# Feature derivatives written in place, and the key and value gradients of layer 0 transposed by DMA

## The chip, the cores and the metric

The kernel runs on one core of a Trainium2 chip. The metric is the device time of one launch in microseconds (us), as the median of several runs. Engines are named as in the profile: PE is TensorE's matmul (PEld its weight load), DVE is VectorE, ACT is ScalarE, POOL is GpSimd, SP is SyncE, which here issues every DMA. L983 means line 983 of the kernel before.

## The reference

A stack of four pre-norm attention layers over 2048 tokens of width 640 (32 heads of 20), and its whole backward pass. Layers 0 and 2 (kind A) are linear attention, layers 1 and 3 (kind B) sliding-window softmax attention with a window of 256. Kind A, cut to what matters:

```
phi = lambda t: where(t > 0, t + 1, exp(t)) + 1e-6
pq, pk = phi(q), phi(k)
kv  = einsum("bhsd,bhse->bhde", pk, v);  z = sum of pk over s
num = einsum("bhqd,bhde->bhqe", pq, kv); den = einsum("bhqd,bhd->bhq", pq, z) + 1e-6
o   = num / den;   x = x + o @ wo      (input of each layer is layernorm(x))
```

Outputs are the result and the gradients of x and of the four weight matrices. The derivative of phi can be had from its stored value: it is exp(t) for t below zero and 1 above, so it equals min(phi - 1e-6, 1). The gradients of q and k before phi are the gradients behind it times that derivative.

## The kernel before

Tokens are cut into 16 tiles of 128 rows. The program runs forward, then the backward pass of layer 3, layer 2, layer 1 and layer 0; the weight gradients (products over all 2048 tokens of two layers, `weight_jobs`) fill in from the end of layer 1 on and then run alone until the end.

The order of the work on PE, DVE, ACT and POOL is written out by hand. Each step of a tile has a place, a number of slots; the step at place a of tile t goes into slot 8t + a (rounded down), and the slots are emitted one after the other, so that steps of neighbouring tiles interleave. Every engine takes its instructions in that order. The DMAs on SP's queue are ordered by the compiler's scheduler, and SP too is in order: a DMA that waits holds up those behind it. PSUM tiles come from a ring of six buffers in order of allocation.

`plan_linear` holds the backward pass of a linear layer for one tile. It is used twice: for layer 2 (with `by_pe` = 0), and for layer 0 (with `by_pe` = 4), where after each slot `fill(0.8)` emits 0.8 us worth of weight-gradient products (eight of 240 columns). The list `PLACES["l2"]` gives its places: first the load, then the steps in the order of `fs`. The steps of a tile are:

- load (for two tiles at once): `ldn`, `lv`, `lpqk` (stored features phi(q) and phi(k)), `lhn`, `lg`, two buffers each;
- `turn`: transposes on PE of `ldn`, `lv` and the key half of `lpqk`, evicted by DVE (`dnT`) and ACT (`vT`, `pkT`);
- `part`: products per half of the heads. For q ("dn") and k ("v") DVE forms the derivative `fd` from `lpqk` (L969) and multiplies the PSUM result by it into `dqa` (L971), two instructions for each of four halves; for v ("pk") ACT copies (L966). `dqa` is the tile's gradient of q, k and v, 128 x 1920, with two buffers;
- `turn_q`, `turn_kv(1)`, `turn_kv(2)`: `dqa` is transposed into `dqT` (three buffers). The q third goes by a DMA transpose, apart from tiles 0 to 3 of layer 0, where PE does it (L921). The k and v thirds go by PE, five transposes each (L983), evicted by DVE (L986) and ACT (L988). Behind the last, `dqa` is stored;
- `dh`: 30 products of `dqT` with the turned weights, for each half first the k third, then v, then q; ACT evicts (L1001);
- `ln`, `ln2`: the layer norm's backward: DVE (L1009, L1011), POOL (L1012), ACT (L1018), POOL (L1019), and for every second tile a store of `lgn`.

The softmax here doesn't subtract the row's maximum and nothing guards it: scores larger than these inputs give would overflow.

## Time and profile before

| What | Value |
|---|---|
| Median of 7 runs | 2253.94 us (2244.75 to 2260.27) |
| The profiled execution | 2250.06 us |
| Its span, first to last instruction | 2248.3 us |
| Mean granted PE clock | 0.981 |
| PE busy over the span | 2073.9 us (92%) |
| DVE, ACT, POOL busy | 1455.0 (65%), 1357.4 (60%), 1091.1 us (49%) |
| Layer 2, backward | about 1168 to 1285 us |
| Layer 0, backward, with weight gradients between | about 1815 to 2030 us |
| Weight gradients alone | about 2030 us to the end |

A row of a group of instructions names the line, the engine, the operation, the tile written and those read, the shapes and the count, then busy time and the mean of one. In the timeline a row has start, duration, the instruction, and in brackets the idle time before it and what ended that. Matmul ends are modelled, so that start to start is the better measure of what a matmul takes in a stream.

### The profile page before, as it was taken

To read this page: it belongs to the slowest core of one execution; us is meant where nothing else is said; L and a number is where in the kernel's file an instruction comes from. 1 tells how busy PE (TensorE), PEld (TensorE's weight loads), DVE (VectorE), ACT (ScalarE), POOL (GpSimd) and SP (SyncE) were. 2 spreads that over 40 slices of the span, in tenths; PEclk is the share of its full clock that TensorE was granted. 3 is DMA by queue.
4 is the path that set the end of the run, shared out by engine and by line. 5 is a ranking of instruction groups with operands and counts; after the bars stand their busy time and mean duration, and the time that the engine had idled before them with its cause. 6 is when DMAs were issued, how large, how long until landed. Compare 5 with 4: busy or idle time off the path is not lost. (4 is left out here: it accounts for less than half of the span.)

```text
span 2248.3 us, 76829 instructions
## 1 busy us (share of the span) xinstructions
PE 2073.9 (92%) x32061; PEld 1692.7 (75%) x32061; DVE 1455.0 (65%) x2934; ACT 1357.4 (60%) x2109; POOL 1091.1 (49%) x1888
## 2 busy tenths in 40 slices
PE   7889998899989999998879989999988899999999
PEld 5667776577767877776657768777776788889998
DVE  6788885777745788887749858788876245540000
ACT  5468887377776888887636668888876234430000
POOL 2056665156666677777534456777775312220000
PEclk9999999999999999999999989999999999999999
DMA  7498875698878599998789733999997998857753
GB/s 260 141 241 226 227 224 150 164 223 220 207 217 223 150 185 208 212 213 174 149 284 256 211 98 93 202 209 208 209 188 171 271 303 246 252 152 199 202 142 90
DMA packets 721357, 449.50 MB, mean 200 GB/s; under 512 B 461296, under 2 KB 697840, under 8 KB 720624
## 3 DMA queue, kind: packets, MB, share of 16 engines
q1 hardware_dynamic: 721008, 444.58, 78.4%
q8 instruction: 251, 4.11, 0.8%
q14 instruction: 98, 0.80, 0.1%
HBM read 213.09 MB, written 149.82 MB: 161 GB/s over the span
## 5 line engine op out<-in xcount | busy, mean ns | idle before, releaser
L665 DVE TENSOR_TENSOR ds<-dp,e 128x768 bf16<-128x768 f32 (+2 forms) x512 | 463.7, 906 | 173.2 <-PE s L138 60.6
L662 ACT ACTIVATE e<-s 128x768 bf16<-128x768 f32 (+2 forms) x512 | 395.6, 773 | 136.2 <-PE s L138 100.0
L385 ACT ACTIVATE eT<-sT 128x1536 bf16<-128x1536 f32 (+2 forms) x256 | 351.1, 1371 | 130.1 <-PE sT L138 128.8
L138 PE MATMUL wg<-rhs,lhs 128*128 128x240 bf16 (+1 forms) x3840 | 377.2, 257 | 10.1 <-DMA lhs<-o 7.1
L138 PEld LDWEIGHTS <-lhs 128*128 128x128 bf16 x3840 | 340.7, 99 | 22.6 <-DMA lhs<-o 8.2
L674 POOL TENSOR_SCALAR_AFFINE_SELECT e<-e 128x256 bf16<-128x256 bf16 x512 | 208.0, 408 | 249.5 <-ACT e L662 242.3
L138 PEld LDWEIGHTS <-dqT 128*128 128x128 bf16 x1920 | 170.7, 98 | 63.2 <-issue 10.4
L391 POOL TENSOR_SCALAR_AFFINE_SELECT eT<-eT 128x512 bf16<-128x512 bf16 x256 | 162.7, 637 | 107.6 <-ACT eT L385 105.9
L138 PE MATMUL acc<-slabqs,ds 128*128 128x20 bf16 x2880 | 210.2, 172 | 1.9 <-ACT dq L744 0.5
L138 PE MATMUL dp<-slabvT,dT 32*128 32x384 bf16 (+2 forms) x1024 | 168.1, 321 | 44.5 <-DVE ds L665 39.5
L138 PE MATMUL acc<-ds,e 128*128 128x20 bf16 x2880 | 208.2, 171 | 0.0
L138 PEld LDWEIGHTS <-ds 128*128 128x128 bf16 x2880 | 187.9, 96 | 12.2 <-issue 3.9
L678 POOL TENSOR_SCALAR_AFFINE_SELECT e<-e 128x256 bf16<-128x256 bf16 x448 | 196.9, 440 | 0.0
L138 PEld LDWEIGHTS <-e 128*128 128x128 bf16 x2880 | 170.1, 96 | 10.9 <-issue 2.1
L1012 POOL TENSOR_TENSOR dh<-dh,lg 128x640 f32<-128x640 f32 x32 | 51.5, 1610 | 255.6 <-DVE s L1009 255.6
L685 PE MATMUL flip<-ident,ds 128*128 128x128 bf16 x1944 | 170.1, 221 | 3.3 <-DVE ds L772 1.2
L138 PE MATMUL s<-slabkT,slabqT 32*128 32x384 bf16 (+2 forms) x1024 | 168.2, 324 | 4.6 <-ACT dT L797 3.3
L1094 DVE CAST wr<-wg 128x240 bf16<-128x240 f32 (+1 forms) x72 | 27.2, 377 | 223.9 <-PE wg L138 211.5
L1092 ACT CAST wr<-wg 128x240 bf16<-128x240 f32 (+1 forms) x48 | 16.3, 339 | 257.3 <-PE wg L138 243.7
L138 PE MATMUL dense<-WB,hnT 128*128 128x320 bf16 x960 | 164.0, 302 | 3.9 <-DVE o L459 2.4
L138 PE MATMUL dense<-WTA,dqT 128*128 128x320 bf16 x960 | 160.9, 298 | 1.9 <-DMA dqT<-dqa 1.6
L138 PE MATMUL acc<-slabks,dsT 128*128 128x20 bf16 x2880 | 147.0, 171 | 12.2 <-DMA dsT<-ds 12.2
(176 smaller groups left out, 4599.7 us busy)
## 6 DMA issues: line engine op xcount, KB each, us to landing
rhs<-dqkv SPq DMA_DIRECT2D x64, 480.0 KB, 4.9
s<-s SPq DMA_DIRECT2D x32, 768.0 KB, 3.9
T<-T SPq DMA_DIRECT2D x32, 768.0 KB, 3.9
dqkv<-dq SPq DMA_DIRECT2D x16, 960.0 KB, 5.8
dqkv<-dqa SPq DMA_DIRECT2D x32, 480.0 KB, 5.0
slabkT<-T SPq DMA_DIRECT2D x56, 256.0 KB, 4.4
slabvT<-T SPq DMA_DIRECT2D x56, 256.0 KB, 3.8
slabks<-s SPq DMA_DIRECT2D x56, 256.0 KB, 3.7
```

Of the source, the lines that this page charges most:

```text
L138: return self.nc.tensor.matmul(out, lhsT=lhsT, rhs=rhs, start=start, stop=stop, skip_group_check=True, **kw)
L385: nc.scalar.activation(e[:, :, 0:nb * P], s[:, :, 0:nb * P], ACT.Exp)
L391: nc.gpsimd.affine_select(out=dg, in_=dg, compare_op=ALU.is_ge, fill=0.0, base=0, pattern=[[0, 4], [1, P]], channel_multiplier=-1)
L662: nc.scalar.activation(u.e[:, :, 0:u.cw], s[:, :, 0:u.cw], ACT.Exp)
L665: nc.vector.tensor_tensor(out=d.ds[:, :, 0:d.cw], in0=d.dp[:, :, 0:d.cw], in1=d.e[:, :, 0:d.cw], op=ALU.mult)
L674: nc.gpsimd.affine_select(out=dg, in_=dg, compare_op=ALU.is_ge, fill=0.0, base=0, pattern=[[0, 2], [-1, P]], channel_multiplier=1)
L678: nc.gpsimd.affine_select(out=fr, in_=fr, compare_op=ALU.is_ge, fill=0.0, base=-1, pattern=[[0, 2], [1, P]], channel_multiplier=-1)
L685: nc.tensor.transpose(ps[:, 3 * j + i, :], f.ds[:, j, i * P:(i + 1) * P], self.ident)
L1012: nc.gpsimd.tensor_tensor(out=x["dh"], in0=x["dh"], in1=L["g"][:, i, :], op=ALU.add)
L1092: nc.scalar.copy(o[:, 0:w], ps[:, 0:w])
L1094: nc.vector.tensor_copy(o[:, 0:w], ps[:, 0:w])
```

## The change

In `part` the two-instruction form for q and k becomes one multiplication by the loaded feature tile, which by then holds the derivative. A new step `slope` turns the q half and the k half of `lpqk` into derivatives in place, one instruction of 640 columns each, at places 0.05 and 0.1. Since that overwrites phi(k), the transposes of phi(k) move from place 1.2 to place -0.6, ahead of those of `lv`. The constant `one` goes. In layer 0, from tile 4 on, `turn_kv` issues a DMA transpose from SP's queue in place of five PE transposes and an eviction, and the places of `dh`, `ln` and `ln2` of these tiles move back by five slots.

```diff
-    l2=[-10.4, -1.3, 0.6, 1.2, 1.9, 3.2, 4.6, 6.2, 7, 7.5, 5, 8, 8.3, 10.2, 11.8, 14, 14.4, 15.4, 16, 16.2, 18.7],
+    l2=[-10.4, -1.3, 0.6, -0.6, 1.9, 3.2, 4.6, 6.2, 7, 7.5, 5, 8, 8.3, 10.2, 11.8, 14, 14.4, 15.4, 16, 16.2, 18.7, 0.05, 0.1],
...
-        self.one = const.tile([P, 1], BF, name="one")
-        nc.gpsimd.memset(self.one, 1.0)
...
-                f = lp.le.tile([P, CW], BF, name="fd")
-                nc.vector.scalar_tensor_tensor(out=f, in0=src("pq" if nm == "dn" else "pk")[:, c * CW:(c + 1) * CW], scalar=-EPS,
-                                               in1=self.one.to_broadcast([P, CW]), op0=ALU.add, op1=ALU.min)
-                nc.vector.tensor_tensor(out=dst, in0=ps[:, 0:CW], in1=f, op=ALU.mult)
+                nc.vector.tensor_tensor(out=dst, in0=ps[:, 0:CW], in1=src("pq" if nm == "dn" else "pk")[:, c * CW:(c + 1) * CW], op=ALU.mult)
+
+        def slope(nm):
+
+            nc.vector.tensor_scalar(out=src(nm), in0=src(nm), scalar1=-EPS, scalar2=1.0, op0=ALU.add, op1=ALU.min)
...
         def turn_kv(j):
+            if lp.by_pe and t >= 4:
+                self.dma(x["dT"][:, j * DT:(j + 1) * DT, :], x["dqkv"][:, j * D:(j + 1) * D], transpose=True)
+                if j == 2:
+                    self.dma(self.rows(self.dq[l], t), x["dqkv"])
+                return
...
-        fs += [lambda n=n, ci=ci: dh(n, ci) for ci in range(2) for n in range(3)] + [ln, ln2]
+        fs += [lambda n=n, ci=ci: dh(n, ci) for ci in range(2) for n in range(3)] + [ln, ln2, lambda: slope("pq"), lambda: slope("pk")]
+        if lp.by_pe and t >= 4:
+            a = a[:13] + [v + 5 for v in a[13:21]] + a[21:]
```

In the built program PE has 120 matmuls fewer, DVE 76 instructions fewer, ACT 12 fewer and SP 24 DMA transposes more.

## The prediction

> **What bounds the kernel now.** I read the page's busy times first (PE 92% of the span), then the chain of work that ended last, then busy time by stretch for the two stages that the change touches, then their timelines and groups. From about 1853 us on, the chain is PE alone (start, length, work):

> ```profile
> 1877.36 1.64 PE wg L138 x16
> 1879.00 1.52 PE dense L138 x14
> ...
> 1890.50 1.64 PE wg L138 x16
> 1892.14 1.52 PE dense L138 x14
> ```

> The pattern repeats every 13.14 us: one tile of layer 0 with 64 weight-gradient products in it. Busy time by stretch, layer 0 from tile 4 on and then layer 2 (us, each engine's busy time with its count, granted clock, DMA share, GB/s):

> ```profile
> 1853.00:2010.70 157.70, 157.70 (x1718) 140.66 (x1717) 89.66 (x170) 62.88 (x130) 37.09 (x24) 1.00 0.79 218
> 1181.90:1283.00 101.10, 94.76 (x1103) 75.94 (x1102) 94.48 (x180) 69.82 (x140) 45.72 (x32) 1.00 0.86 234
> ```

> In layer 0 PE never idles and DVE is at 57%. In layer 2 DVE is busy as long as PE, 94.5 of 101.1 us, and PE idles 6.3. The PE timeline of layer 2 shows why:

> ```profile
> 1230.59 0.51 PE L162 MATMUL flip<-ident,ldn 128*126 128x128 bf16 x6
> ...
> 1237.73 0.51 PE L162 MATMUL flip<-ident,ldn 128*126 128x128 bf16 x6
> ...
> 1239.53 0.32 PE L138 MATMUL dense<-dmz,pkT 120*128 120x40 bf16 x4 [0.45 <-DVE dqa L971]
> ```

> A tile takes 7.1 to 7.3 us there (from 1179.92 to 1252.22 the same row comes ten times further on, 7.23 us each), and in each a product waits for a PSUM buffer that DVE empties late. Without a wait a tile takes 6.58 us: two of the ten intervals are that long (1179.92 to 1186.50, 1216.68 to 1223.26), and the layer 0 tile gives the same, 13.14 less 64 products at 0.82/8 us.

> DVE is late because of L969. Its groups in layer 2:

> ```profile
> L969 DVE SCALAR_TENSOR_TENSOR fd<-lpqk,one 128x320 bf16<-128x320 bf16 x56 | 47.4, 846 | 0.0
> L971 DVE TENSOR_TENSOR dqa<-dense,fd 128x320 bf16<-128x320 f32 x55 | 27.0, 492 | 5.5
> ```

> L969 is half of DVE's busy time. Alone it takes 0.48 us; where POOL's sums L1012 or L1019 run it takes 1.1 to 1.8 us and ends some 0.35 us after POOL does (1237.55 + 1.33 = 1238.88; POOL's ended at 1238.53). L971 is 0.49 us whether POOL runs or not.

> **Derivative in place.** Removed per tile: 4 x 0.846 = 3.4 us of DVE. Added: two instructions of 128x640 with one bf16 source. No such row exists; the nearest are L417 (same size, bf16, 435 to 447 ns, up to 741) and L560 (half the size, in place, 244 ns). I take 0.44 each, 0.9 a tile, and for the bounds 0.23 and 1.5 us each (stretched by POOL as L969 was; at slot 8t POOL is idle in layer 2, as it waits for L1009 behind them). DVE's load falls from 94.48/14 = 6.75 to about 4.3 us a tile, well below 6.58, so the PSUM wait goes. The multiplication reads the same sizes: no change. In layer 0 the freed 2.5 us a tile is worth nothing: PE waits for DVE nowhere in the stretch.

> What is late next in layer 2? Three candidates. (a) DVE now has to wait, in `slope` of k, for PE's transposes of phi(k); behind it are L1009 and the evictions. Those transposes stand a slot earlier on PE (place -0.6 against 0.1), and DVE's previous instruction, the eviction L986, already waits for later PE work; cost 0. (b) The eviction L986 has less PE work to hide behind, since the phi(k) transposes no longer stand there: k-v transposes start at 0, eviction runs from 0.48 to 0.97 us (1897.16, 1897.64, 1898.13 in layer 0), and its reader can come at 0.55 + 0.34 + 0.15 = 1.04 us. It just fits: 0 to 0.1 us a tile. (c) The q transpose. For odd tiles SP's queue has it behind the store of `lgn`, and that ends the chain L1009, L1012, L1018, L1019. Before: L1019 ends at 1238.53, the transpose is issued at 1239.02, lands 3.7 us later (the stage's median) at about 1242.7, and is read by the products at 1243.46: 0.7 us to spare. The two slopes stand ahead of L1009 and push the chain back by 0.9, less some 0.2 that DVE gains; the reader comes 0.5 us earlier in a shorter tile (six slots of eight). So it is about 0.5 us late in every odd tile. The even tiles' transposes wait for the multiplications only, which come over 1 us earlier. The phi(k) load has about 9 us of slack and needs 1.6.

> Sum for layer 2: 14 tiles x (7.23 - 6.58) = 9.1 us, less 7 x 0.5 for (c), about 6 us. Bounds: 9.5, and 2 if (c) costs a full microsecond in every odd tile.

> **Key and value gradients by DMA, layer 0.** Removed from PE: 12 tiles x 10 transposes. In the stream ten take 0.55 us from start to start, not the modelled 0.72:

> ```profile
> 1897.16 0.72 PE L983 MATMUL flip<-ident,dqa 128*128 128x128 bf16 x10
> 1897.71 0.51 PE L162 MATMUL flip<-ident,lv 128*126 128x128 bf16 x6
> ```

> 12 x 0.55 = 6.6 us, all on the path, as PE is never idle there. The weight products are a fixed total, so five more slots at the end only move them. The evictions L986 (0.49) and L988 (0.69 us) that go were beside PE's work: 0.

> Added: 24 transposes on SP's queue and the DMA engines. SP takes 1.24 us for one (median of the q ones), 2.5 us of a 12.6 us tile; behind them stand the `dqa` store, loads and the stores of weight gradients, whose tiles have slack. The new wait is of the first `dh` product for the k third. In the built order I counted PE's work between the last product that feeds a k or v transpose, with all that stands ahead of it on SP, and the reader: at least 11 us at the durations above. Needed: about 0.75 us on DVE or ACT, 1.2 to 3.7 of SP, and the landing, whose row is

> ```profile
> DMA to landing us min/median/max: 2.6/4.1/7.1
> ```

> At the median that is hidden; with the longest landing and three transposes in a row (0.75 + 3.7 + 7.1 = 11.6) it is 0.6 us late. So the DMA engines decide. One transpose alone, in a DMA window of 1.2 us (672 packets, 640 of them its own):

> ```profile
> q1 hardware_dynamic: 672, 0.16, 68.7%
> ```

> 0.687 x 1.2 = 0.82 us of all 16 engines; 24 make 20 us. Amid other traffic the packets of one took up to 2.8 us of engine time in the trace's records, but that includes sharing. The stage has 0.79 x 157.7 = 124.6 us; with 20 more, 144.4 in 157.7 - 6.6 = 151.1 us, a share of 0.96; from 1900 to 1920 us the share is 1.10 with PE busy for all 20 us. I take 0.5 us lost in all (one late landing), 6 us won. Bounds: 6.6 won, and the loss below.

> [...]

> **Sum.** 6 + 6 = 12 us off 2250.06 (the profiled execution, 1.8 of it outside the span) is 2238; the median of the runs stands 3.9 above that execution, so 2253.94 - 12 = 2242.

> **Rivals.**
> *Both in full* (part of my case): 9.1 + 6.6 = 15.7 us, 2238.
> *One gain is taken by a new wait* (0.19): either (c) costs a microsecond or more, so that the transposes replace DVE as the bound of layer 2, or the k and v transposes are late by 0.5 us a tile in layer 0. Then 6 us are left: 2248, at the edge of "same". For it: four waits for `dqT` already (3.5 us) in layer 2. Against: the even tiles' transposes come earlier.
> *The DMA engines become the bound of layer 0* (0.08), the other side. The stage then takes 124.6 + 24 x C us. Above C = 1.1 us it exceeds PE's 151.1; at C = 2.0 it eats layer 2's gain too, and above that the kernel is slower. At 2.5, near what transposes took amid traffic, it is 184.6 us, 27 longer than now, less 6: 2275. For it: a share of 0.79 already, small packets. Against: 0.82 alone.
> *The change doesn't do what it says*: excluded by the built order (120 PE transposes and 76 DVE instructions fewer, 24 DMA transposes more).

> **How the numbers follow.** Forecast 0.73 (2234 to 2247), one gain lost 0.19 (2245 to 2252), DMA bound 0.08 (2250 to 2280). About 0.3%, 6.8 us, is what a measurement of this kernel can tell from no change. Faster: 0.73 and a little of the second case, 0.75. Same: the rest of the second and a little of the third, 0.16. Slower 0.09. Range 2233 to 2253: down to both gains in full with the medians' scatter, up to the second case.

> **What would show it.** Right: `ldn` transposes of layer 2 some 6.6 to 6.9 us apart with no wait for `dqa L971`; tiles of layer 0 12.6 us apart with PE busy throughout; slopes at about 0.44 us. Wrong: PE waiting for `dqT<-dqa` in either stage for more than some 5 us, a DMA share near 1.1 over the whole of layer 0, or a longer wait for `lhs<-o` behind it (2.0 us now).

## The result and the profile after

| | Before | After |
|---|---|---|
| Median of the runs, same chip | 2253.8 us | 2243.16 us (2236.06 to 2245.81) |
| Ratio of after to before, 95% interval | | 0.9947 [0.9935, 0.9960] |
| The profiled execution | 2250.06 us | 2243.45 us |
| Its span | 2248.3 us | 2241.7 us |
| Mean granted clock | 0.981 | 0.976 |

The kernel is faster by 0.53%, 11.9 us by the ratio (9.0 to 14.7). The forecast was 12 us. The sum came out; the experiments show that its two terms did not. The gain in layer 0 was sized wrongly, and the runs give the other part more than its 6 us.

First the two stretches of before again, in the kernel after (us, busy time of PE, PEld, DVE, ACT, POOL with counts, granted clock, DMA share, GB/s; layer 2 first):

```profile
1181.90:1283.00 101.10, 97.05 (x1129) 78.38 (x1128) 57.83 (x154) 69.84 (x143) 41.45 (x32) 1.00 0.86 235
1853.00:2010.70 157.70, 157.70 (x1667) 140.30 (x1664) 56.00 (x136) 56.24 (x121) 35.25 (x24) 1.00 1.00 249
```

In layer 2 DVE goes from 94.48 busy us to 57.83. PE still idles 4 of 101 us, but for another reason. What its products waited for in these 101 us (total, times, longest), before:

```profile
PE dense L138 <- DVE dqa L971: 4.8, 11, 0.5
...
PE dense L138 <- DMA dqT<-dqa: 1.6, 2, 1.1
```

and after:

```profile
PE dense L136 <- DMA dqT<-dqa: 4.0, 5, 1.6
```

The wait for DVE's multiplication is gone, and the wait for the q transposes has grown. In layer 0 PE is busy throughout as before, while the DMA share goes from 0.79 to 1.00. Since PE doesn't wait there, the spacing of the tiles tells the gain. The chain of waits, where before had 13.14 us from one pattern to the next:

```profile
1881.11 1.64 PE wg L136 x16
1882.75 1.52 PE dense L136 x14
...
1893.72 1.64 PE wg L136 x16
1895.37 1.52 PE dense L136 x14
```

1893.72 - 1881.11 = 12.61 us. The PE timeline of layer 2:

```profile
1201.95 0.51 PE L160 MATMUL flip<-ident,ldn 128*126 128x128 bf16 x6
...
1208.69 0.51 PE L160 MATMUL flip<-ident,ldn 128*126 128x128 bf16 x6
...
1211.05 0.88 PE L987 MATMUL flip<-ident,dqa 128*128 128x128 bf16 x10
1211.77 0.51 PE L160 MATMUL flip<-ident,lv 128*126 128x128 bf16 x6
...
1215.41 0.85 PE L136 MATMUL dense<-WTA,dqT 128*128 128x320 bf16 x5 [1.33 <-DMA dqT<-dqa]
...
1216.94 0.51 PE L160 MATMUL flip<-ident,ldn 128*126 128x128 bf16 x6
```

A tile of 6.74 us, then one of 8.25, in which the `dh` products wait for the q transpose. Five such waits, of 0.16 to 1.6 us and all in odd tiles, make the 4.0 us. DVE's groups in layer 2, the multiplication (L971 before, L966 in the kernel after) and the new slope:

```profile
L966 DVE TENSOR_TENSOR dqa<-dense,lpqk 128x320 bf16<-128x320 f32 x56 | 25.6, 485 | 9.7 <-PE dense L136 9.6
...
L970 DVE TENSOR_SCALAR lpqk<-lpqk 128x640 bf16<-128x640 bf16 x28 | 7.7, 318 | 0.0
```

The multiplication is as it was (485 against 492 ns); the slope takes 318 ns, not the 440 I had put in.

What layer 0 gives is partly taken back behind it. The weight gradients alone begin with a gap on PE, for left operands (`lhs`) that have not landed. The PE timeline there, before:

```profile
2069.94 6.24 PE L138 MATMUL wg<-rhs,lhs 128*128 128x160 bf16 x64 [2.01 <-DMA lhs<-o]
```

and after:

```profile
2060.25 0.45 PE L136 MATMUL wg<-rhs,lhs 128*128 128x160 bf16 x4 [0.72 <-DMA lhs<-o]
2062.06 0.45 PE L136 MATMUL wg<-rhs,lhs 128*128 128x160 bf16 x4 [1.36 <-DMA lhs<-o]
2063.79 2.45 PE L136 MATMUL wg<-rhs,lhs 128*128 128x160 bf16 x17 [1.28 <-DMA lhs<-o]
```

In brackets is the idle time ahead of each row and what ended it: 2.0 us in one piece before, 3.4 in three after. (By starts, so with the weight load that waits first, PE's gap is 2.24 us before and 4.05 after; gaps below are meant so.)

At the border of layer 2 and layer 1 PE waits some 3 us once, in both kernels, but before ahead of layer 1's first pair of `s` products (its attention scores) and after ahead of the second. Before:

```profile
1296.48 0.29 PE L138 MATMUL s<-slabkT,slabqT 32*128 32x128 bf16 x2 [3.27 <-ACT dT L797]
```

and after:

```profile
1295.55 0.29 PE L136 MATMUL s<-slabkT,slabqT 32*128 32x128 bf16 x2 [3.07 <-ACT e L660]
```

So layer 2 is measured to the second pair, behind this wait in both. By stage (start to start of named PE products, one profile each, us):

| | Before | After |
|---|---|---|
| Layer 2: first `ldn` transpose to layer 1's second pair of `s` products | 134.4 | 131.3 |
| Layer 1: from there to the first weight product | 466.1 | 467.2 |
| Layer 0: first `ldn` transpose to last `dh` | 217.75 | 214.56 |
| From there to the last weight product | 218.9 | 216.1 |

Other profiles with the same instructions in layer 2 as after have 127.9 to 131.3 us for it. So a single profile settles a stage to a few us only, and the verdicts below are by the ratios of many runs, with the traces for the mechanism.

### The profile page after: what moved, and what is told of

It is laid out like the page before. It is cut to its first block, busy times and chain, and to the rows that moved or that the text cites. A ratio compares the mean times of both kernels' runs of the same rounds, so it can differ in the third digit from the quotient of the medians.

```text
span 2241.7 us, 76479 instructions
## 1 busy us (share of the span) xinstructions
PE 2076.0 (93%) x31941; PEld 1693.7 (76%) x31941; DVE 1374.1 (61%) x2858; ACT 1347.6 (60%) x2097; POOL 1082.8 (48%) x1887
## 5 line engine op out<-in xcount | busy, mean ns | idle before, releaser
L136 PE MATMUL wg<-rhs,lhs 128*128 128x240 bf16 (+1 forms) x3840 | 377.4, 257 | 11.5 <-DMA lhs<-o 9.0
L136 PEld LDWEIGHTS <-lhs 128*128 128x128 bf16 x3840 | 340.2, 99 | 26.3 <-DMA lhs<-o 10.4
L136 PEld LDWEIGHTS <-dqT 128*128 128x128 bf16 x1920 | 170.9, 98 | 65.9 <-issue 10.4
L136 PEld LDWEIGHTS <-ds 128*128 128x128 bf16 x2880 | 187.9, 96 | 12.6 <-issue 4.4
L1016 POOL TENSOR_TENSOR dh<-dh,lg 128x640 f32<-128x640 f32 x32 | 44.8, 1399 | 245.0 <-DVE s L1013 168.4
L136 PE MATMUL dense<-WTB,dqT 128*128 128x320 bf16 x960 | 155.6, 302 | 0.0
```

The source lines that it names most:

```text
L136: return self.nc.tensor.matmul(out, lhsT=lhsT, rhs=rhs, start=start, stop=stop, skip_group_check=True, **kw)
L1016: nc.gpsimd.tensor_tensor(out=x["dh"], in0=x["dh"], in1=L["g"][:, i, :], op=ALU.add)
```

## The experiments

The theory going in: the slopes free DVE, which gives layer 2's gain; the q transposes are the next wait there, as part (c) of the prediction has it; in layer 0 the gain is PE's, with transposes hidden by the five slots' lead, and some of it is lost in the gap behind it. The rivals: the two parts give other shares than 6 and 6 (e1, e2); the q transposes are late for the slopes (e3), for the store ahead of them on SP's queue (e11, e12, e13), or for their landing alone; those of layer 0 are hidden without the lead too (e4), or only just (e6); the gap is noise (e8 to e10). All ratios are to the kernel before on the same chip.

**Each part alone.** e1_slope is the kernel after without the second part:

```diff
-            if lp.by_pe and t >= 4:
+            if lp.by_pe and t >= 99:
                 self.dma(x["dT"][:, j * DT:(j + 1) * DT, :], x["dqkv"][:, j * D:(j + 1) * D], transpose=True)
...
-        if lp.by_pe and t >= 4:
-            a = a[:13] + [v + 5 for v in a[13:21]] + a[21:]
```

> The derivative in place alone (both layers), the k and v thirds of dqa still transposed on PE, dh at its old places. Theory (two separate gains, about 5 us in layer 2 from the DVE load that goes, about 6 us in layer 0 from PE transposes that go): the layer 2 gain alone, 2249 us (ratio 0.998), the span of layer 2 shorter by 3 to 6 us, layer 0 unchanged at 13.14 us a tile. Rival (the layer 2 gain is given back in layer 1, all of the result comes from layer 0): 2254 us, ratio 1.000.

Measured: 0.9961 [0.9949, 0.9973], 8.8 us less (6 to 11.5), more than the 5 expected. Layer 2 takes 127.9 us in its profile, where before has 134.4.

e2_kv is the kernel before with the branch in `turn_kv` and the shift of five slots, and the old derivative:

```diff
         def turn_kv(j):
+            if lp.by_pe and t >= 4:
+                self.dma(x["dT"][:, j * DT:(j + 1) * DT, :], x["dqkv"][:, j * D:(j + 1) * D], transpose=True)
+                if j == 2:
+                    self.dma(self.rows(self.dq[l], t), x["dqkv"])
+                return
...
+        if lp.by_pe and t >= 4:
+            a = a[:13] + [v + 5 for v in a[13:21]] + a[21:]
```

> The k and v transposes by DMA with dh five slots later in layer 0 alone; the derivative is formed by the old two-instruction form. Theory: layer 0's gain alone, 6 us, 2248 us (ratio 0.9973), 12.6 us a tile in layer 0, layer 2 as before at 7.23 us a tile. Rival (all of the result comes from layer 0): 2243 us, ratio 0.995. Second rival (DVE with its old load of 2.5 us more a tile evicts dqa too late for the DMA transposes): over 2250 us, PE waits for dqT in layer 0.

Measured: 0.9993 [0.9978, 1.0008], 1.6 us less, which is no difference that these runs can tell; the 0.9973 expected lies outside. Layer 0 has no wait for a transpose in it. The gap behind it is there again, longer:

```profile
2064.03 0.45 PE L138 MATMUL wg<-rhs,lhs 128*128 128x160 bf16 x4 [1.24 <-DMA lhs<-o]
2065.82 0.58 PE L138 MATMUL wg<-rhs,lhs 128*128 128x160 bf16 x4 [1.35 <-DMA lhs<-o]
2067.60 8.62 PE L138 MATMUL wg<-rhs,lhs 128*128 128x160 bf16 x86 [1.20 <-DMA lhs<-o]
```

and so is what follows from it. The same view by stretch as above, for 12 us at the gap in e2_kv:

```profile
2062.00:2074.00 12.00, 8.22 (x77) 7.51 (x75) 0.33 (x1) 0.29 (x1) 0.00 (x0) 0.72 0.85 233
```

The granted clock is 0.72 on average over the 12 us. If it was 0.50 for a part of them and 1.00 else, as behind the gaps of before and after, that makes an estimate of 6.7 us at half clock (12 x 0.28 x 2). The two parts together (after) give 11.9; alone they sum to 10.4, equal within the intervals. So by the ratios the slope carries three quarters of the gain, not half.

**What delays the q transposes of layer 2?** e3_late puts the slopes behind L1013 (L1009 before) on DVE, so that they no longer push the chain to the store of `lgn`:

```diff
-... 16.2, 18.7, 0.05, 0.1],
+... 16.2, 18.7, 0.25, 0.3],
```

> The changed kernel with the two slope steps at places 0.25 and 0.3, behind L1013 (the layer norm's sum on DVE, place 0.2) instead of ahead of it; nothing else moves. Theory (c) of the prediction (the slopes push back the chain that ends with the store of lgn, and SP has the q transpose behind that store): L1013 starts 0.55 us sooner, and PE's waits for dqT in layer 2, 4.0 us in the changed kernel's trace, fall to 1 or 2: 2 to 3 us less than the changed kernel, ratio about 0.9935. Rival (these waits come from the DMA engines' load, not from the chain): waits and time as the changed kernel's, ratio 0.9945 to 0.9947.

Measured: 0.9931 [0.9914, 0.9947]; after's 0.9947 lies at the end of that, so no difference is shown. The DVE timeline says why the chain hardly moves:

```profile
1211.84 0.49 DVE L990 COPY dqT<-flip 128x640 bf16<-128x640 bf16 x1 [1.38 <-PE flip L987]
1212.49 0.83 DVE L1013 CUSTOM_DVE_ANT_0 lna<-dh,lhn 128x640 f32<-128x640 f32 x1 [0.16 <-ACT dh L1005]
...
1213.37 2.10 DVE L970 TENSOR_SCALAR lpqk<-lpqk 128x640 bf16<-128x640 bf16 x2
```

With the slopes out of the way L1013 waits for ACT's eviction of `dh`, so it starts only about 0.2 us earlier in its tile than in after, and the store goes out 0.1 us earlier. The slopes now run beside POOL's sums, and the two together take 1.8 to 2.1 us from start to end, where they took 0.55. PE waits 4.5 us for the q transposes, against 4.0. Taking the slopes out of the way doesn't bring the transposes earlier.

e11_store is e8_lhs (below) with layer 2's store of `lgn` issued from POOL's queue, off SP's:

```diff
-                self.dma(self.pair(g_out, t // 2), L["gn"])
+                if l == 2:
+                    with nc.allow_non_contiguous_dma(reason="tiled layouts"):
+                        nc.gpsimd.dma_start(out=self.pair(g_out, t // 2), in_=L["gn"])
+                else:
+                    self.dma(self.pair(g_out, t // 2), L["gn"])
```

> The changed kernel with the earlier loads of the left operand and, in layer 2, the store of lgn issued from POOL's queue (behind L1023, which makes it) and not from SP's. Theory (in odd tiles the q transpose is late because SP holds it behind that store): the transpose is issued about 1.2 us sooner, PE's waits for dqT in layer 2 fall from 3.7 us to under 1, ratio 0.9905 against 0.9919. Rival (the landing of 4 to 5 us is set by the DMA engines' load in those tiles, or POOL's issue of the store delays its own chain by over 1 us): no gain, 0.992 or more.

Measured: 0.9978 [0.9964, 0.9992], against 0.9919 [0.9902, 0.9935] for e8_lhs: slower by 13 us. Layer 1's first load of `g` reads what the stores wrote, and waits on SP's queue until the store has landed. This wait (total, times, longest) in e8_lhs, from 1190 to 1222 us:

```profile
SPq L106 <- DMA g<-lgn: 0.3, 1, 0.3
```

and in e11_store, from 1190 to 1225 us:

```profile
SPq L106 <- DMA g<-lgn: 5.1, 1, 5.1
```

In e8_lhs the store lands 3.5 us after its issue (1192.76, 1196.24), when SP has just come to the load. From POOL's queue it takes 6.0 (1196.64, 1202.68), and SP stands still for most of that. Behind the load stands the next q transpose, issued at 1204.18 where after has 1200.70. PE waits 7.5 us for transposes in the stretch. So this edit lengthens another wait, and doesn't tell the theories apart.

SP's timeline in after tells more:

```profile
1207.99 0.36 SPq L106 DMA_DIRECT2D lg<-g  x1
1208.44 0.42 SPq L106 DMA_DIRECT2D lhn<-hn  x1
1209.62 0.36 SPq L106 DMA_DIRECT2D g<-lgn  x1
1210.07 1.32 SPq L106 DMA_TRANSPOSE dqT<-dqa  x1
```

By DVE's timeline the q gradient is whole at about 1207.4 (the second of three multiplications from 1206.54 on). The transpose then stands behind the load of `lg`, which waits for POOL's sum L1016 (to 1207.97), and the store, which waits for L1023 (to 1209.59). It is issued 2.6 us after its data is there, and is the one that PE waits 1.33 us for. e12_put is e8_lhs with the store as a step of its own at place 21.4, so that the transpose goes ahead of it, on the same queue:

```diff
-            if i == 1:
-                self.dma(self.pair(g_out, t // 2), L["gn"])
+        def put():
+            self.dma(self.pair(g_out, t // 2), X[t // 2]["gn"])
...
-        return ([(a[0], load)] if i == 0 else []) + list(zip(a[1:], fs))
+        PUT = 21.4 if l == 2 else a[20]
+        return ([(a[0], load)] if i == 0 else []) + list(zip(a[1:], fs)) + ([(PUT, put)] if i == 1 else [])
```

> e8_lhs with the store of lgn as a step of its own, emitted 2.7 slots later (place 21.4), so that on SP's queue it stands behind the q transpose of an odd tile of layer 2, with no new queue as in e11_store. Still ahead of that transpose: the loads lg and lhn of the next pair, of which lg waits for POOL's sum L1016. If the queue's order makes the transposes late, those of odd tiles are issued some 1.1 us earlier (1208.9 on after's clock, where after has 1210.07), PE's waits for dqT in layer 2 fall from about 4 us to about 1, and the ratio to before goes from 0.9919 to about 0.9907. If landing decides, landings get longer by what the issue gains, the waits stay at 3 to 5 us, and the ratio stays at 0.992.

Measured: 0.9916 [0.9899, 0.9933], no difference from e8_lhs that the intervals show. But PE's wait falls as the theory of the queue said. PE's waits in layer 2, e8_lhs:

```profile
PE dense L136 <- DMA dqT<-dqa: 3.7, 3, 1.6
```

and e12_put:

```profile
PE dense L136 <- DMA dqT<-dqa: 1.4, 3, 0.8
```

From 1214 to 1262 us all its tiles are 6.74 us apart (one in e8_lhs takes 7.64), while landings are as long (median 4.6 us, 4.8 in e8_lhs). The six profiles with after's layer 2 have waits of 2.1 to 4.0 us, so 1.4 lies below them all, but in one profile. e13_three is e12_put with a third buffer for `lg` and `lhn`, so that their loads don't wait for POOL:

```diff
-                L[nm] = self.load(pool, "l" + nm, self.pair(src, t // 2), [P, 2, w])
+                L[nm] = self.load(pool, "l" + nm, self.pair(src, t // 2), [P, 2, w], **(dict(bufs=3) if l == 2 and nm in ("g", "hn") else {}))
```

> e12_put with three buffers instead of two for lg and lhn of layer 2, so that their loads no longer wait for POOL's sum. The data of an odd tile's q transpose is there at about 1207.4 on after's clock; if the queue decides, the transpose is issued within half a microsecond of that, 2.5 us earlier than in after, no wait for dqT longer than 0.3 us is left, tiles of layer 2 are 6.74 us apart throughout, and the ratio is about 0.990. If landing decides, waits of 3 to 5 us stay and the ratio is 0.992.

Measured: 0.9927 [0.9908, 0.9945]. PE waits 2.2 us, twice, where no wait over 0.3 was expected; the transpose that it waits 1.6 us for was issued 6.6 us before its reader could have started (1200.34, 1206.98), between layer 1's first loads, and took 8.2 us to land. So the queue's order accounts for the waits of odd tiles in these traces, and landing for the one that is left here. By the ratios neither is worth more than the runs can tell.

e7_kv2 goes after the 0.16 us by which a free tile of layer 2 (6.74) misses the 6.58. The ten k and v transposes take 0.72 us from start to start in it (1211.05 to 1211.77 above), not 0.55: PEld waits 2.3 us in 14 times for ACT's copy of the v gradient, L964. e3_late with those of v half a slot later:

```diff
-... 7, 7.5, 5, 8, 8.3, 10.2, ...
+... 7, 7.5, 5, 8, 8.65, 10.2, ...
```

> As the run with late slopes, and the transposes of the v third of dqa at place 8.65 instead of 8.3, so that PE does the six transposes of lv between those of k and those of v. Theory (a tile of layer 2 without waits takes 6.74 us, not 6.58, because the ten transposes take 0.72 us: those of v wait 0.16 for ACT's eviction L964, which has only the dh products to hide behind): ten transposes back at 0.55, a tile at 6.58 us, 16 x 0.16 = 2.6 us less than with late slopes alone, ratio about 0.9925. Rival (the wait moves to the evictions behind it): as late slopes alone.

Measured: 0.9946 [0.9928, 0.9964], nothing won. The waits of layer 2 in e7_kv2 (total, times, longest):

```profile
PE dense L136 <- ACT dqT L992: 4.0, 13, 0.4
...
PE dense L136 <- DMA dqT<-dqa: 0.4, 2, 0.3
```

The wait for L964 is replaced by one for the eviction of the same transposes, L992, of 0.3 us a tile; a tile now takes 7.05 us. The waits for the q transposes nearly go, in a longer tile.

**How much room have the transposes of layer 0?** e6_twice issues each of the 24 new ones twice, into the same place:

```diff
                 self.dma(x["dT"][:, j * DT:(j + 1) * DT, :], x["dqkv"][:, j * D:(j + 1) * D], transpose=True)
+                self.dma(x["dT"][:, j * DT:(j + 1) * DT, :], x["dqkv"][:, j * D:(j + 1) * D], transpose=True)
```

> The changed kernel with each of the 24 new k and v transposes issued twice into the same place (same output, 24 transposes more). Theory (a transpose costs 0.82 us of the DMA engines in effect, the stage has a few us to spare): 20 us more of DMA time on top of a stage that shows a DMA share of 1.00, and two more issues of 1.24 us on SP ahead of each reader; PE waits appear, 5 to 15 us in all, 2248 to 2258 us. Rival A (there is much room on the DMA engines, the share of 1.00 is only sharing): 2243 to 2245 us. Rival B (the engines are full at a share of 1.00): all 20 us and more come through, 2263 us or over.

Measured: 1.0093 [1.0064, 1.0123], 33 us more than after, in the range of rival B. Busy time by stretch, PE's wait, and a wait of SP's queue that after doesn't have, e6_twice:

```profile
1853.00:2030.00 177.00, 160.03 (x1620) 140.13 (x1619) 55.59 (x135) 56.30 (x119) 34.99 (x24) 0.96 0.94 231
```

```profile
PE dense L136 <- DMA dqT<-dqa: 17.0, 7, 4.9
```

```profile
SPq L106 <- DMA dqT<-dqa: 18.2, 10, 4.5
```

PE waits 17 us for transposes, up to 4.9 at once, and the granted clock, 0.96 over these 177 us, can have cost up to 7 more: 24 of the 27 us by which layer 0 is longer than after's in its profile. But the second of two transposes into one place waits on SP's queue until the first has landed, 18.2 us in all, so that two landings come one behind the other. And the DMA share is 0.94, less than after's 1.00. So this run doesn't show that the DMA engines were full; how much room they had stays open.

e4_noshift is after without the shift of `dh`, `ln` and `ln2`:

```diff
-        if lp.by_pe and t >= 4:
-            a = a[:13] + [v + 5 for v in a[13:21]] + a[21:]
```

> The changed kernel without the shift of dh, ln and ln2 by five slots: the same DMA transposes with 5.3 us of PE work, at the trace's durations, between the last product that feeds them and their reader, instead of 11 us and more. Theory (the lead hides the transposes; about 0.75 us of eviction, 1.2 to 2.5 of SP issue and 4.3 of landing are needed, 6.5 to 8 us): PE waits 1 to 3 us in each of 12 tiles, 12 to 36 us, 2255 to 2280 us, slower than before. Rival (the DMA transposes land early enough anyway and the shift does nothing): 2243 us.

Measured: 0.9997 [0.9985, 1.0010], 11 us more than after. PE's wait, e4_noshift:

```profile
PE dense L136 <- DMA dqT<-dqa: 8.2, 7, 1.7
```

With 5.3 us of PE's work ahead of the reader instead of 11 the transposes are late, seven times, for less than the 12 to 36 us expected. In after no product waits for them; the lead is needed.

**What does the shift cost?** It holds the last `dh` back by five slots, and with each slot go eight weight products, so 40 of them (4.1 us) run before layer 0's end that ran behind it. PE's products from the last `dh` to the first wait, before:

```profile
2026.27 41.66 PE L138 MATMUL wg<-rhs,lhs 128*128 128x240 bf16 x414
```

and after:

```profile
2022.51 37.01 PE L136 MATMUL wg<-rhs,lhs 128*128 128x240 bf16 x366
```

In that time SP issues the loads of the next left operands, eight pieces of 640 KB, a few of them early and the rest together. These last ones (start, duration, count), before:

```profile
2057.01 3.20 SPq L108 DMA_DIRECT2D lhs<-o  x5
```

after:

```profile
2049.24 5.68 SPq L106 DMA_DIRECT2D lhs<-o  x6
```

and in e4_noshift:

```profile
2051.00 2.99 SPq L106 DMA_DIRECT2D lhs<-o  x5
```

Five late pieces before and six after: in the shorter time SP gets two out early, not three. PE's waits after end 1.8 and 1.7 us apart, each for a further piece, so one late piece more is about the 1.8 us by which the gap is longer (4.05 less 2.24). e4_noshift has the transposes by DMA without the shift: five late pieces, and a gap of 1.9 us. All five traces with the shift and without the earlier loads (after, e2, e3, e6, e7) have six, and gaps of 4.05 to 4.6. So the shift, and not the transposes, makes the gap longer. Why one piece fewer goes out early, these traces don't show. e8_lhs is after with the loads asked for at the first product group of the job before, not at its third:

```diff
+            early = None
+            if k + 1 < len(todo) and todo[k + 1][3] == 0 and not W.tight:
+                early = [lhs(a) for a in todo[k + 1][0]]
             for m in range(DT):
...
-                    nxt = [lhs(L2[0]), None if W.tight else lhs(L2[1])], nxt[1]
+                    nxt = early or [lhs(L2[0]), None if W.tight else lhs(L2[1])], nxt[1]
```

> The changed kernel with the loads of the next left operand (lhs<-o, and later lhs<-hn) asked for at the first of the five products of the job before, not at the third: 17 us of PE work between the order and the use instead of 10.4. Theory (the shift by five slots took 4.1 us of cover from these loads; PE waits 4.0 us for them in three pieces where it waited 2.2 before the change, and its granted clock then falls to half for 3.4 to 6.8 us, so that layer 0's gain of 6.6 shrinks to some 3): no such gap, no halved clock at that place, 4 to 6 us less than the changed kernel, 2238 us, ratio to before about 0.9925. Rival (the gap is made up elsewhere, the small gain of the DMA transposes has another cause): 2243 us, ratio 0.9945.

Measured: 0.9919 [0.9902, 0.9935], 18 us less than before and 6.3 less than after: with e12_put the fastest of all. The last loads are issued at

```profile
2036.78 6.48 SPq L106 DMA_DIRECT2D lhs<-o  x6
```

and no product waits for them; four waits of 0.3 to 0.9 us are left, three of them for the right operands (`rhs`). Ten us around the gap by stretch, e8_lhs:

```profile
2050.00:2060.00 10.00, 7.83 (x96) 7.10 (x94) 0.73 (x2) 0.29 (x1) 0.00 (x0) 1.00 0.89 214
```

The clock stays at 1.00, where the same ten us of after (from 2058 on) have 0.83 and PE busy for 6.64. To see to which part this belongs, the same edit was put on e2_kv (e9_kv_lhs) and on e1_slope (e10_slope_lhs).

> The DMA transposes alone (old two-instruction derivative) with the same earlier loads of the left operand. Theory: with that gap away the transposes give what PE saves, 6 to 8 us (6.6 of transposes and up to 2 for the gap that the kernel before has there too): ratio about 0.997. Rival (the DMA transposes cost as much in layer 0 as they save, whatever stands behind): ratio 0.999 as without the earlier loads.

> The derivative in place with the earlier loads of the left operand, k and v thirds transposed on PE and dh at its old places: what the run with these loads and the DMA transposes (ratio 0.9919) has without the transposes. Theory (with the gap behind layer 0 away, the transposes are worth what PE saves, 6.6 us, on top of the derivative): ratio 0.9945 to 0.9955, 6 to 8 us slower than with the transposes. Rival (the derivative and the earlier loads do all of it): ratio 0.992.

Measured: 0.9962 [0.9949, 0.9974] for e9_kv_lhs, where e2_kv had 0.9993 [0.9978, 1.0008]: 7 us less. And 0.9953 [0.9936, 0.9969] for e10_slope_lhs, where e1_slope had 0.9961: 1.8 us less, within the intervals. By the ratios the earlier loads are worth 6 to 7 us where the transposes go by DMA and `dh` is shifted, and little where it isn't. With them the transposes bring 7.6 us (0.9919 against 0.9953, intervals that all but touch) or 8.6 (e9_kv_lhs, with what the loads bring by themselves in it). The profiles show less of it: layer 0 to the end is 4.1 us shorter in e8_lhs than in e10_slope_lhs, and where the rest lies one profile each can't say. Nor do the earlier loads always close the gap: in e9_kv_lhs's profile, an execution of 2253.08 us where the median is 2244.62, PE stands idle at that place for right operands (2.14, 0.26 and 0.46 us), and the 27 products behind these waits take 3.38 us, where in e12_put the next 143 take 10.05.

## Why the prediction was right, and where it was not

**Layer 2: the mechanism right, the size only roughly.** DVE was the bound, and PE's wait for L971 went. A free tile takes 6.74 us, in the range of 6.6 to 6.9 that was given as the sign. The predicted gain was 6. Over the six profiles with after's layer 2 unaltered the stage takes 129.5 us on average (127.9 to 131.3), over the three with the old derivative 134.4 (134.1 to 134.8): 4.9 less. The runs give the slope more: 8.8 (6 to 11.5) by itself, and about 10 as the difference of after and e2_kv or of e8_lhs and e9_kv_lhs. Against before's profile e1_slope's wins 2.0 of it behind layer 0, where its gap of 1.9 us brings no halved clock. Where the rest lies is open. The terms that were off:

- The slope, 0.44 us by L417, took 0.318. Why L417, of the same size and type, takes longer (medians of 435 to 446 ns), these runs don't show. The error was small, as DVE had about 2.5 us a tile to spare either way.
- The lateness (c), 3.5 us by the sum, is 2.1 to 4.0 in the six profiles (3.1 on average). The "four waits (3.5 us)" that before was said to have were two, of 1.6 us on PE: that view counts each once on PE and once on its weight load. The place held: with the transpose ahead of the store (e12_put) less is left, 1.4. What the sum had push the store back did not hold: with the slopes behind L1009 (e3_late) the store comes 0.1 us earlier, as ACT's eviction holds the chain, and the wait stays.
- The 6.58 of a free tile leaves out 0.16 us for L964 (14 times, 2.3 us), a term put at nothing; candidate (b), the eviction's reader, "just fits" in after and is what stops e7_kv2.

**Layer 0: right within the stage.** 12.61 us a tile where the sum had 12.6, PE never idle, and no wait for a k or v transpose. The rival in which the DMA engines become the bound did not come; the share is 1.00 in after and 0.97 in e8_lhs, both with these transposes and their lead, where the sum had 0.96. How far off it was stays open, since e6_twice holds up SP's queue as well. By the rival's own sum layer 2's gain is eaten at C = 1.6 us (124.6 + 24 x 1.6 = 163.0, against 157.7 + 6), not at 2.0.

**The step that failed: "The weight products are a fixed total, so five more slots at the end only move them."** They are, but where they move from they had covered a transfer. From after against e1_slope, whose layer 0 differs by this part alone: up to the last `dh` 2.9 us less (6.6 for the transposes, less 4.1 for the moved products, makes 2.5), behind it 0.8 less. The 4.1 moved out should be there; instead PE's gap is 4.05 us against 1.9 (the measure of before's 2.24), and in the stretch at half clock 20 products take 0.133 us in place of 0.068, which adds 1.3. So 2.15 + 1.3 = 3.4 us are taken back, of some 6.6, and 2.9 + 0.8 = 3.7 are left, to about 1 us (e10_slope_lhs, with e1_slope's layer 0, is 0.9 shorter up to the last `dh`). The runs say 3.2 on top of the slope (0.9947 against 0.9961, a difference within the intervals) and 1.6 alone. The step was priced at 0, with the sign "a longer wait for `lhs<-o`" named for the case that it was wrong: that sign is what came.

So by the runs 12 = 6 + 6 stood for about 8.8 + 3.2. That the two errors cancel is luck.

## What to carry to other kernels

A shift that only moves filler work may not be free: ask which transfer that filler was covering where it is taken from, and ask for that transfer earlier in the same change (here 6.3 us, for four lines). Test a change's parts alone even when the sum comes out as forecast. Where a transfer is late, compare the time its data was ready with its issue, and change the order on its queue before moving work to another: in their profiles e12_put took more than half of PE's wait away (3.7 to 1.4 us), and e11_store made another one longer (SP's, 0.3 to 5.1). And when a stage is measured between two products, make sure that a wait at the border lies on the same side in both kernels: here 3 us changed sides.

## What the hardware showed unexpectedly

The same transpose by DMA cost the DMA engines 0.82 us alone. In layer 0 the share over 157.7 us rose from 0.75 (e1_slope) to 1.00 (after) and from 0.75 (e10_slope_lhs) to 0.97 (e8_lhs). For some 24 transposes that makes an estimate of 1.4 to 1.6 us each, up to twice as much. The recorded time includes sharing (before's share from 1900 to 1920 us is 1.10, more than the engines' whole time), so it bounds the cost from above.
